# Block order, LayerNorm statistics and early GLU weights in an attention and GLU kernel on one NeuronCore

## The chip, the cores and the metric

The kernel runs on one core of a Trainium2 chip. Five engines work in parallel, each on its own list of instructions in order: TensorE (PE), VectorE (DVE), ScalarE (ACT), GpSimd (POOL) and SyncE (SP), which here only starts DMA transfers. They wait for one another through semaphores. The metric is the device time of one execution in microseconds (us).

## The reference

The input is one sequence of S = 2048 tokens with D = 576 channels, float32. First comes an attention layer, then a gated MLP, each behind a LayerNorm without scale or shift and each added to its input:

```
h  = x + softmax(q k^T * 18**-0.5 over the keys s, s-2, .. s-14) v @ wo    q, k, v = layernorm(x) @ wqkv, 32 heads of 18
h2 = h + (sigmoid(n @ w_gate) * (n @ w_up)) @ w_down                       n = layernorm(h), F = 4608
```

## The kernel before, in words

**Blocks.** A key lies an even number of tokens back, so even and odd tokens never meet. Each half of them is cut in two, which gives four blocks of 512 tokens (0 and 1 even, 2 and 3 odd). A block is held as four token tiles of 128 (the loops over j). The 32 heads are four groups g of 8 (144 channels).

**Precision.** Each product is built of fp32r matmuls: an operand is split into a high part (a copy on ACT, L104) and a low part (the rest, a subtraction on DVE, L105), and three products are summed. L108 and L109 do the same for the last 64 channels. A split is thus always an ACT instruction and a DVE instruction that waits for it.

**The front half** (up to some 223 us). For a block, SP loads x (`load_x`); `ln1` normalizes each token tile with `ln_j`, transposes it on PE (`tr_main`, `tr_rest`) and splits it into the operands th and tl. `ln_j` takes mean and variance with bn_stats and bn_aggr on DVE (L123, L124), the power -1/2 on POOL (L126), and applies them on DVE (L134, L135) or, for blocks 2 and 3, on ACT (L130 to L132). `qkv(b, g)` is four passes (one for each j) of 14 matmuls of 432 columns; the results are evicted by ACT (L384, to ev) and stored to DRAM from ACT's DMA queue (L388, L390).

**Attention** is a generator (`att_all`) that VectorE works off piece by piece while PE runs the passes: for each (block, group) in the order (0,0), (0,1), (1,0), (0,2), (0,3), (1,1), (1,2), (1,3) it loads q, kw and vw (L169 to L171, SP), then does two products pr (L182) and their sums lg (L186), mx, sub, Exp on ACT (L194 to L196), and the weighted sum of v (L208 to L219). `step(ag, n)` lets it advance n pieces for each qkv pass. Blocks 2 and 3 have their attention later, under the GLU. For block 0 the result is a tile of tokens; for the others it is stored by POOL (L221) and loaded again (oj, L570).

**The order of qkv passes** is written out by hand: `norm_under(b, xb, call, n)` interleaves the norm of block b with the passes of `call`, and `heads` lists the passes that follow. `raw_w` and `qkv_w` load and split the weights of a group.

**`front`** then projects block 0 by wo, adds x, normalizes and builds the GLU operands of block 0. It runs between the last qkv passes, (2,3) and (3,3). Its last act is a store of the transposed block (`x<-tok`, ACT queue, L505).

**The GLU** runs over 108 items (a weight chunk for one block or for a pair of blocks; the first 14 are chunks for block 0 alone). An item of the first kind is two products b of 14 matmuls, a sigmoid on ACT (L653), a product on DVE (L629) and a split into h0h and h0l, then the down projection dp (L723). Its weights come as one row of 928 KB (wg), which `weights` splits into w1, w4, w2 and the down part d one item ahead, and `load_gu` loads two items ahead. Chunk 0 is an exception: it is loaded into a tile of the front half (wg0) and `first_split` splits it there to wf, since the pools of the GLU (gw, gd and others) take over memory of the front half (tok, x, weights) and must wait until it is free. A tile in reused memory waits for the last reader of what lay there.

**Background.** While items run, attention (1,2) and (1,3), and after that the projection of block 1 (transposes of oj, L139), go on in their gaps.

**What sets the order within an engine.** A scheduler places instructions by their order in the code and by `tc.high_priority`: a higher number lifts the instructions in it over others that could go at that point.

Of the kernel before, what the change touches and what calls it, by code (L numbers as in the profile page):

```python
# [15 lines left out]
F32 = mybir.dt.float32  # L16
# [5 lines left out]
P = 128  # L22
# [38 lines left out]
def kernel(ctx, tc, x, wqkv, wo, wmlp, out):  # L61
# [53 lines left out]
                sp.dma_start(bass.AP(tensor=a.tensor, offset=a.offset,  # L115
                                     ap=[[LP * CG // 16, 16], [1, LP * CG // 16]]), zero)

    def ln_j(xj, xn, on_act):
        bs = sm.tile([P, 2, 6], F32, bufs=4, name="bs")
        mv = sm.tile([P, 2], F32, bufs=4, name="mv")  # L120
        rstd = sm.tile([P, 1], F32, bufs=4, name="rstd")
        for k in range(2):
            dve.bn_stats(bs[:, k], xj[:, k * DH2:(k + 1) * DH2])  # L123
        dve.bn_aggr(mv, bs)  # L124
        dve.tensor_scalar(rstd, mv[:, 1:2], EPS, None, ALU.add)
        pool.tensor_tensor(rstd, rstd, mhalf, ALU.pow)  # L126
        if on_act:
            nm = sm.tile([P, 1], F32, bufs=4, name="nm")
            dve.tensor_scalar(nm, mv[:, 0:1], -1.0, None, ALU.mult)
            act.activation(xn[:, :D], xj, AF.Identity, bias=nm)  # L130
            act.activation(xn[:, :D], xn[:, :D], AF.Copy, scale=rstd)
            act.activation(xn[:, D:DX], xn[:, DM:D], AF.Copy)  # L132
        else:
            dve.tensor_scalar(xn[:, :D], xj, mv[:, 0:1], rstd, ALU.subtract, ALU.mult)  # L134
            dve.tensor_copy(xn[:, D:DX], xn[:, DM:D])  # L135

    def tr_main(ps, xn):
        for c in range(4):
# [101 lines left out]
    def proj_j(bank, t, wos, th, tl, xn_tile, put, order=(0, 1)):  # L240
        oj = t[0]
        pv = tr_main(bank(), oj)
        with tc.high_priority(HI):
            split(th[:, 0:4], tl, pv)
        yield
        pv = tr_rest(bank(), oj)
        with tc.high_priority(HI):
            split_rest(th[:, 4], pv)
        yield
        for i in order:  # L250
            ps = bank()
            tok_major(ps, DH2, th, tl, slice(0, P), *wos[i])
            hs = t[1][:, i * DH2:(i + 1) * DH2]
            with tc.high_priority(HI):
                dve.tensor_tensor(hs, hs, ps[:, :DH2], ALU.add)
            yield
        xn = xn_tile()
        with tc.high_priority(HI):
            ln_j(t[1], xn, False)
# [62 lines left out]
    def tok_tile(shape=(P, NS, DX)):  # L322
        return stk.tile(list(shape), F32, tag="tok", bufs=2, name="tok")
# [7 lines left out]
    def load_x(b):  # L331
        e, hf = BLOCKS[b]
        t = sah.tile([P, NS, D], F32, bufs=2, name="h")
        for j in range(NS):
            sp.dma_start(t[:, j], xv[e, hf][:, j])
        return t

    def ln1(b, xb):
        th = th3_tile(F32R) if b == 3 else th_tile()
        tl = tl_tile()  # L340
        yield th, tl
        xn = tok_tile()
        for j in range(NS):
            js = slice(j * P, (j + 1) * P)
            pri = 2 * HI if b == 0 else HI if b > 1 else 0
            with tc.high_priority(pri):
                ln_j(xb[:, j], xn[:, j], b > 1)
# [76 lines left out]
    def norm_under(b, xb, call, n):  # L424
        gl = ln1(b, xb)
        T.append(next(gl))
        for _ in call:
            step(ag, n)
            next(gl, END)
            step(ag, n)  # L430
        drain(gl)

    def heads(order, ws, n):
        for b, g in order:
            for _ in qkv(b, g, T[b], ws[g]):
                step(ag, n)
# [11 lines left out]
    xb = load_x(2)  # L448
    norm_under(2, xb, qkv(1, 0, T[1], w[0]), 1)
    xb = load_x(3)  # L450
    wr = raw_w(2)
    norm_under(3, xb, qkv(2, 0, T[2], w[0]), 1)
    heads(((3, 0),), w, 2)
    w.append(qkv_w(2, wr))
    wr = raw_w(3)
    pads(2)
    heads(((1, 1), (0, 2), (2, 1), (3, 1)), w, 2)
    w.append(qkv_w(3, wr))
    pads(3)
    h = load_x(0)  # L460
# [58 lines left out]
    fr = front()  # L519
    for _ in qkv(1, 3, T[1], w[3]):  # L520
        step(ag, 1 if ready else 4)
    while not ready:
        step(ag, 1)
    more = qkv(2, 3, T[2], w[3])
# [15 lines left out]
                ww = first_split(wg)  # L540
    with tc.high_priority(HI):
        drain(fr)
    ps_stk.close()
    sa_stk.close()

# [429 lines left out]
    items = ([("std", 0, f) for f in range(NSTD)] + [("pair", 0, f) for f in range(NSTD, NF)]  # L975
             + [("std", 1, f) for f in range(NSTD)] + [("pair", 1, f) for f in range(NF)])
    bg = under_first()
    with tc.high_priority(2 * HI):
        wg2 = load_gu(1, pool)
        d = d_tile()  # L980
        split(d[:, 0], d[:, 1], wg[:, GU:WC])
        wc = ww, d
    wg = wg2
    seg = []

    def last_pair(i):
# [123 lines left out]
    for c, (kind, p, f) in enumerate(items):  # L1110
# [11 lines left out]
        if c == NF + NSTD:  # L1122
# [4 lines left out]
            X = Xn  # L1127
            pp_stk.close()
            dw = ctx.enter_context(sb_pool("dw", "right"))
        if c + 1 < len(items):  # L1130
            wc = weights(items[c + 1][0], wg, c + 1 < NF + NSTD)
        if c + 2 < len(items):
            wg = load_gu(items[c + 2][2], n=WC if c + 2 < NF + NSTD else GU)
# [94 lines left out]
```

## Time and profile before

| | us |
|---|---|
| three timed runs | 1587.89, 1590.72, 1589.88 (median 1589.88) |
| profiled execution, from its first to its last instruction | 1589.2 |
| TensorE busy in it | 1553.3 |
| VectorE busy | 1268.1 |
| ScalarE busy | 869.2 |

The profile is one execution of its own, and the trace gives its span as its time. A row of the timeline has a start, a length, the engine, the line of the kernel, the operation, the tile written <- the tiles read, their shapes, and how many instructions of the same kind follow each other; in brackets stands the idle time of the engine just before and what ended it. PEld are weight loads, which run beside PE's matmuls; SPq, ACTq and POOLq are DMA issues on these engines' queues. PEclk is the granted clock of TensorE as a share of the full one.

### The profile page before, as it was taken

How to read it: one execution, taken by the hardware profiler on the slowest of the kernel's cores; microseconds unless marked ns; L12 is line 12 of the kernel's file. 1: busy time of each engine (PE TensorE's matmuls, PEld its weight loads, DVE VectorE, ACT ScalarE, POOL GpSimd, SP SyncE). 2: the span in 40 equal slices, each digit the busy share in tenths (PEclk: the TensorE clock that was granted, in tenths of full speed). 3: DMA queues.
4: the chain of work that ended last, by engine and by line, in shares of the span. 5: the costliest groups of instructions: out<-in, count | busy, mean ns of one | idle time of the engine just before them, and what ended most of it. 6: DMA issues, size and time to landing. Idle time of an engine off the chain costs nothing.

```text
span 1589.2 us, 22383 instructions
## 1 busy us (share of the span) xinstructions
PE 1553.3 (98%) x8532; PEld 1381.6 (87%) x8532; DVE 1268.1 (80%) x1931; ACT 869.2 (55%) x1546; POOL 184.2 (12%) x230
## 2 busy tenths in 40 slices
PE   7999979999999999999989999999999999999998
PEld 6999968888888888888879988888888888888887
DVE  7999988959999999999546687876677776677755
ACT  4432234425555666656443255776677776677761
POOL 1000000011010001000101100122112112212210
PEclk9999999999999999999999999999999999999999
DMA  7664544346367565665764234899989999989983
GB/s 267 208 206 163 193 184 165 133 177 246 104 164 205 157 170 139 166 191 149 210 203 143 100 110 110 182 186 181 176 169 183 184 173 180 177 170 182 184 170 124
DMA packets 76892, 273.50 MB, mean 172 GB/s; under 512 B 8336, under 2 KB 14224, under 8 KB 75888
## 3 DMA queue, kind: packets, MB, share of 16 engines
q0 software_dynamic: 27792, 105.89, 36.3%
q1 hardware_dynamic: 41360, 146.06, 27.4%
q10 hardware_dynamic: 7632, 20.12, 3.3%
q8 instruction: 67, 1.10, 0.3%
q14 instruction: 41, 0.34, 0.1%
HBM read 145.88 MB, written 128.52 MB: 173 GB/s over the span
## 4 chain that ended last, share of the span: by engine, by line
PE 55%; issue 27%; POOL 7%; DVE 6%; DMA 4%; ACT 1%; SPq 0%; POOLq 0%; ACTq 0%; DVEq 0%
PE b L609 23%; PE dp L723 15%; POOL h L794 7%; PE acc L150 6%; PE b L616 4%; PE b L150 1%; PE bgp L150 1%; DMA wg<-in_wmlp_dram 1%; DVE pr L182 1%; DMA x<-tok 1%; DVE pr L208 1%; DVE lg L186 1%; PE acc L152 1%; DMA tail<-h 1%; PE acc L153 1%
## 5 line engine op out<-in xcount | busy, mean ns | idle before, releaser
L609 PE MATMUL b<-tl,w 128*128 128x512 f32 x1716 | 438.1, 395 | 9.1 <-ACT w L104 6.5
L609 PEld LDWEIGHTS b<-tl,w 128*128 128x128 f32 x1716 | 311.7, 189 | 66.5 <-ACT w L104 7.7
L609 PE MATMUL b<-th,w 128*128 128x512 f32 x1368 | 352.8, 393 | 0.4 <-DVE s L698 0.3
L609 PEld LDWEIGHTS b<-th,w 128*128 128x128 f32 x1368 | 249.8, 188 | 46.7 <-DVE s L698 0.7
L104 ACT ACTIVATE w<-wg 128x640 fp32r<-128x640 f32 (+2 forms) x197 | 117.0, 598 | 125.2 <-PE b L616 59.8
L791 ACT ACTIVATE ev<-dp 128x576 f32<-128x576 f32 x224 | 145.0, 647 | 61.8 <-PE dp L785 58.2
L616 PE MATMUL b<-th,w 128*128 128x512 f32 x572 | 177.0, 391 | 0.0
L794 POOL DMA_DIRECT2D h<-ev x128 | 110.2, 862 | 456.8 <-ACT ev L791 440.5
L105 DVE TENSOR_TENSOR w<-wg,w 128x640 fp32r<-128x640 f32 (+2 forms) x197 | 126.8, 649 | 38.7 <-ACT w L104 38.3
L150 PE MATMUL acc<-qw,th 128*128 128x432 f32 x512 | 155.7, 365 | 1.2 <-DVE th L109 0.9
L105 DVE TENSOR_TENSOR w<-tw,w 128x512 fp32r<-128x512 f32 x116 | 79.6, 687 | 81.1 <-ACT w L104 80.2
L616 PEld LDWEIGHTS b<-th,w 128*128 128x128 f32 x572 | 107.7, 188 | 23.1
L723 PE MATMUL dp<-d,h0h 128*128 128x288 f32 x640 | 119.0, 296 | 1.7 <-DVE tail L733 1.7
L723 PE MATMUL dp<-d,h1h 128*128 128x288 f32 x640 | 120.0, 297 | 0.0
L723 PEld LDWEIGHTS dp<-d,h0h 128*128 128x128 f32 x640 | 99.4, 189 | 5.5 <-DVE tail L733 2.0
L150 PEld LDWEIGHTS acc<-qw,th 128*128 128x128 f32 x512 | 97.2, 190 | 6.5 <-DVE th L109 1.1
L723 PEld LDWEIGHTS dp<-d,h1h 128*128 128x128 f32 x640 | 99.5, 190 | 2.9
L731 ACT ACTIVATE stage<-dp 128x576 f32<-128x576 f32 x96 | 61.7, 646 | 62.4 <-PE dp L723 62.3
L104 ACT ACTIVATE w<-tw 128x512 fp32r<-128x512 f32 x116 | 72.8, 628 | 41.3 <-PE b L609 40.9
L150 PE MATMUL acc<-qw,tl 128*128 128x432 f32 x256 | 92.8, 362 | 0.0
L384 ACT ACTIVATE ev<-acc 128x432 f32<-128x432 f32 x64 | 33.9, 531 | 104.4 <-PE acc L153 97.7
L182 DVE TENSOR_TENSOR pr<-kw,q 128x2304 f32<-128x2304 f32 x32 | 81.7, 2552 | 2.8 <-DMA kw<-k 2.6
(278 smaller groups left out, 2899.8 us busy)
## 6 DMA issues: line engine op xcount, KB each, us to landing
h<-ev POOLq DMA_DIRECT2D x96, 576.0 KB, 7.2
wg<-in_wmlp_dram SPq DMA_DIRECT2D x49, 928.0 KB, 5.2
h<-stage POOLq DMA_DIRECT2D x24, 1152.0 KB, 10.6
wg<-in_wmlp_dram SPq DMA_DIRECT2D x36, 640.0 KB, 4.1
kw<-k SPq DMA_DIRECT2D x16, 792.0 KB, 4.4
vw<-v SPq DMA_DIRECT2D x16, 792.0 KB, 5.5
wd<-in_wmlp_dram SPq DMA_DIRECT2D x18, 576.0 KB, 7.2
h<-ev POOLq DMA_DIRECT2D x32, 288.0 KB, 6.8
```

The lines of the kernel that those rows point to most:

```text
L104: act.activation(hi, src, AF.Copy)
L105: splits.append(dve.tensor_tensor(lo, src, f32(hi), ALU.subtract))
L150: pe.matmul(ps[:, :n], a[:, c, js], m[:, c], start=k == 0, stop=False)
L152: pe.matmul(ps[:, :n], th[:, 4, js], wh[:, 4], start=False, stop=False)
L182: dve.tensor_tensor(pr, both(kw, u), q[:, us].unsqueeze(2).broadcast_to([P, 2, W, CG]), ALU.mult)
L384: act.activation(ev[:, :, j], ps[:, :NQ].rearrange("p (t c) -> p t c", t=3), AF.Copy)
L609: pe.matmul(ps, wt[:, a, k0 + c], xx[:, m + c], start=first and k == 0, stop=k == 5, skip_group_check=True)
L616: pe.matmul(ps, wt[:, a, k0], xx[:, 4], start=False, stop=a == 1, skip_group_check=True)
L723: pe.matmul(ps[:, i, :DH2], a[:, js], d[:, m, i * DH2:(i + 1) * DH2], start=k == 0, stop=k == n)
L731: act.activation(hv, ps, AF.Copy)
L791: act.activation(hs[:, k % 2], ps[:, :, :DH2], AF.Copy)
L794: pool.dma_start(hsev[:, u, k0:k + 1], hs[:, :k + 1 - k0], accum_op=ALU.add, max_dma_last_dim=8 * D)
```

## The change

It has three parts.

1. **Norm statistics of blocks 2 and 3 go to ScalarE.** The new `ln_stats` takes the negative mean (a Copy with accum_out) and the sum of squared deviations (a Square with accum_out) on ACT, then three small operations on POOL. `ln_scale` applies them in one ACT instruction (Identity with bias and scale) and copies the last 64 channels. Statistics are issued one token tile ahead; the priority of this work falls from HI to 0. bn_stats, bn_aggr and two small DVE operations per token tile go.
2. **qkv(1,1) runs under the norm of block 3** instead of qkv(2,0), and qkv(2,0) follows it; the raw weights of group 2 are loaded after that norm's loads in the code.
3. **Chunk 1 of the GLU is handled like chunk 0.** Its row is loaded on SP into a tile "h" of the front half, after the passes of (1,3) are emitted, and split (`first_split`) before the front's stacks close. The down parts of chunks 0 and 1 are split there too, into tiles df. The POOL-queue load of chunk 1 and the split of chunk 0's d in gd go; the loop takes the ready weights for chunk 1.

```diff
+    def ln_stats(xj, junk):
+        mv = sm.tile([P, 2], F32, bufs=4, name="mv")
+        rstd = sm.tile([P, 1], F32, bufs=4, name="rstd")
+        act.activation(junk[:, :D], xj, AF.Copy, scale=-1.0 / D, accum_out=mv[:, 0:1])
+        act.activation(junk[:, :D], xj, AF.Square, bias=mv[:, 0:1], accum_out=mv[:, 1:2])
+        pool.tensor_scalar(rstd, mv[:, 1:2], 1.0 / D, EPS, ALU.mult, ALU.add)
+        pool.tensor_tensor(rstd, rstd, mhalf, ALU.pow)
+        pool.tensor_tensor(mv[:, 0:1], mv[:, 0:1], rstd, ALU.mult)
+        return mv[:, 0:1], rstd
+
+    def ln_scale(xj, nr, xn):
+        act.activation(xn[:, :D], xj, AF.Identity, bias=nr[0], scale=nr[1])
+        act.activation(xn[:, D:DX], xn[:, DM:D], AF.Copy)
...
     xb = load_x(3)
+    norm_under(3, xb, qkv(1, 1, T[1], w[1]), 1)
     wr = raw_w(2)
-    norm_under(3, xb, qkv(2, 0, T[2], w[0]), 1)
-    heads(((3, 0),), w, 2)
+    heads(((2, 0), (3, 0)), w, 2)
     w.append(qkv_w(2, wr))
     wr = raw_w(3)
     pads(2)
-    heads(((1, 1), (0, 2), (2, 1), (3, 1)), w, 2)
+    heads(((2, 1), (0, 2), (3, 1)), w, 2)
...
     for _ in qkv(1, 3, T[1], w[3]):
         step(ag, 1 if ready else 4)
+    with tc.high_priority(HI):
+        wg1 = sah.tile([P, NS, D], F32, bufs=2, name="h").rearrange("p j d -> p (j d)")[:, :WC]
+        sp.dma_start(wg1, wmlp[1])
...
+    def first_down(ws):
+        d = xt.tile([P, 2, D], F32R, tag="tl", bufs=4, name="df")
+        split(d[:, 0], d[:, 1], ws[:, GU:WC])
+        return d
+
+    with tc.high_priority(HI):
+        wc = ww, first_down(wg)
+        wc_next = first_split(wg1), first_down(wg1)
     ps_stk.close()
     sa_stk.close()
...
-    with tc.high_priority(2 * HI):
-        wg2 = load_gu(1, pool)
-        d = d_tile()
-        split(d[:, 0], d[:, 1], wg[:, GU:WC])
-        wc = ww, d
-    wg = wg2
...
-        if c + 1 < len(items):
+        if c == 0:
+            wc = wc_next
+        elif c + 1 < len(items):
             wc = weights(items[c + 1][0], wg, c + 1 < NF + NSTD)
```

How this moves instructions shows best at three places. The rows name the line, the operation and tile<-tiles; lines of the new kernel differ from the old, so L182 of before is L189 now, L186 is L193, L653 is L678.

On SP, where the front half issues the loads of blocks 2 and 3 (h<-in_x_dram) and of the first attention (q, kw, vw), before:

```order
14 L335 DMA h<-in_x_dram 128x576 x4
15 L362 DMA wr<-in_wqkv_dram 128x432 x5
16 L115 DMA k_2_77<-zero 16x63
17 L115 DMA v_2_85<-zero 16x63
18 L115 DMA k_2_81<-zero 16x63
19 L115 DMA v_2_89<-zero 16x63
20 L115 DMA k_3_78<-zero 16x63
21 L169 DMA q<-q_0_91 128x576
22 L170 DMA kw<-k_0_75 128x1584
23 L171 DMA vw<-v_0_83 128x1584
24 L335 DMA h<-in_x_dram 128x576 x4
```

and now:

```order
14 L342 DMA h<-in_x_dram 128x576 x4
15 L375 DMA wr<-in_wqkv_dram 128x432 x5
16 L342 DMA h<-in_x_dram 128x576 x4
17 L176 DMA q<-q_0_91 128x576
18 L177 DMA kw<-k_0_75 128x1584
19 L178 DMA vw<-v_0_83 128x1584
```

The loads of block 3 stood behind those of the first attention and now stand ahead of them.

On VectorE, at the start of `front`, where tl is the first low part of the transposed attention result, before:

```order
196 L219 TENSOR_TENSOR tok<-kw 128x4x144
197 L182 TENSOR_TENSOR pr<-kw,q 128x2304
198 L409 COPY tok<-tok 128x64 x4
199 L186 TENSOR_REDUCE lg<-pr 128x128
200 L105 TENSOR_TENSOR tl<-mm,th 128x4x128
```

and now:

```order
173 L226 TENSOR_TENSOR tok<-kw 128x4x144
174 L189 TENSOR_TENSOR pr<-kw,q 128x2304
175 L105 TENSOR_TENSOR wow<-ws,wow 128x288 x2
176 L422 COPY tok<-tok 128x64 x4
177 L193 TENSOR_REDUCE lg<-pr 128x128
178 L189 TENSOR_TENSOR pr<-kw,q 128x2304
179 L193 TENSOR_REDUCE lg<-pr 128x128
180 L201 TENSOR_REDUCE mx<-lg 128x32
181 L202 TENSOR_TENSOR lg<-lg,mx 128x256
182 L105 TENSOR_TENSOR tl<-mm,th 128x4x128
```

Between the tile of tokens and tl stood one lg of attention (1,1); now lg, pr, lg, mx and sub stand there.

On ScalarE, from the store of x to the weights of the item after next, before (d is chunk 0's down part, w_2276 to w_2280 are chunk 1's weights, s is the sigmoid of chunk 0):

```order
180 L505 DMA x_113<-tok 128x2560
181 L384 ACTIVATE ev<-acc 128x3x144
182 L388 DMA q_3_106<-ev 128x576
183 L390 DMA k_3_82<-ev 128x576
184 L104 ACTIVATE d<-wg_2056 128x576
185 L390 DMA v_3_90<-ev 128x576
186 L653 ACT_TABLE_LOAD
187 L653 ACTIVATE s<-b_2291 128x512
188 L104 ACTIVATE w_2276<-wg 128x640
189 L104 ACTIVATE w_2279<-wg 128x384
190 L104 ACTIVATE w_2280<-wg 128x256
```

and now (wf and df<-h are chunk 1's, w_2316 is chunk 2's):

```order
197 L518 DMA x_113<-tok 128x2560
198 L397 ACTIVATE ev<-acc 128x3x144
199 L104 ACTIVATE wf<-h 128x256
200 L401 DMA q_3_106<-ev 128x576
201 L403 DMA k_3_82<-ev 128x576
202 L403 DMA v_3_90<-ev 128x576
203 L104 ACTIVATE wf<-h 128x384
204 L104 ACTIVATE df<-h 128x576
205 L203 ACTIVATE lg<-lg 128x256
206 L678 ACT_TABLE_LOAD
207 L678 ACTIVATE s<-b_2256 128x512
```

Chunk 1's weights stood behind the sigmoid of chunk 0 and now stand ahead of it, and so does an Exp of attention (lg), which stood behind them. On PE, the transposes of oj (L139 before, L146 now) stood at the 1553rd matmul and stand at the 1485th.

More of the change, by code (lines that the diff above doesn't have):

```diff
@@ L116, in pads, with ln_j @@
                                      ap=[[LP * CG // 16, 16], [1, LP * CG // 16]]), zero)
-    def ln_j(xj, xn, on_act):
+    def ln_j(xj, xn):
         bs = sm.tile([P, 2, 6], F32, bufs=4, name="bs")
@@ L126, in ln_j @@
         pool.tensor_tensor(rstd, rstd, mhalf, ALU.pow)
[L127 to L135, printed above, removed]
+        dve.tensor_scalar(xn[:, :D], xj, mv[:, 0:1], rstd, ALU.subtract, ALU.mult)
+        dve.tensor_copy(xn[:, D:DX], xn[:, DM:D])
+    def ln_stats(xj, junk):
[10 more added lines that the diff above has]
+        act.activation(xn[:, D:DX], xn[:, DM:D], AF.Copy)
     def tr_main(ps, xn):
@@ L258, in proj_j @@
         with tc.high_priority(HI):
-            ln_j(t[1], xn, False)
+            ln_j(t[1], xn)
         yield
@@ L342, in ln1 @@
         xn = tok_tile()
+        pri = 2 * HI if b == 0 else 0
+        nr = []
         for j in range(NS):
             js = slice(j * P, (j + 1) * P)
-            pri = 2 * HI if b == 0 else HI if b > 1 else 0
+            while b > 1 and len(nr) < min(j + 2, NS):
+                nr.append(ln_stats(xb[:, len(nr)], xn[:, len(nr)]))
             with tc.high_priority(pri):
-                ln_j(xb[:, j], xn[:, j], b > 1)
+                if b > 1:
+                    ln_scale(xb[:, j], nr[j], xn[:, j])
+                else:
+                    ln_j(xb[:, j], xn[:, j])
             pv = tr_main(mm_tile(), xn[:, j])
```

## The prediction

> **What bounds the kernel now.** I read the page first, then the split of the span into windows, then the list of waits, and last the timeline at the places the list names.
>
> ```profile
> span 1589.2 us, 22383 instructions
> PE 1553.3 (98%) x8532; PEld 1381.6 (87%) x8532; DVE 1268.1 (80%) x1931; ACT 869.2 (55%) x1546; POOL 184.2 (12%) x230
> ```
>
> TensorE is busy for 1553.3 of 1589.2 us, and the diff leaves its matmuls alone. So the change can only move the 35.9 us in which PE stands still, and the stretches in which it runs at a lower granted clock. The list of waits over the whole span says who causes the first (the columns are the total, the count and the longest):
>
> ```profile
> PE b L609 <- ACT w L104: 6.5, 1, 6.5
> PE b L609 <- DVE s L629: 2.5, 1, 2.5
> PE b L139 <- DMA oj<-o: 2.4, 1, 2.4
> ```
>
> The windows of 5 us show the second (PE busy, PEld, DVE, ACT, POOL, then PEclk, DMA share, GB/s):
>
> ```profile
> 235.00:240.00 5.00, 1.46 (x3) 0.78 (x4) 4.93 (x4) 3.59 (x7) 0.00 (x0) 0.50 0.11 41
> 240.00:245.00 5.00, 5.00 (x13) 3.98 (x14) 4.73 (x9) 0.27 (x1) 0.00 (x0) 0.50 0.16 30
> 245.00:250.00 5.00, 5.00 (x22) 4.07 (x21) 1.42 (x3) 3.35 (x6) 0.00 (x0) 0.91 0.42 160
> 250.00:255.00 5.00, 5.00 (x28) 4.39 (x27) 4.97 (x7) 4.09 (x6) 0.00 (x0) 1.00 0.63 215
> 320.00:325.00 5.00, 5.00 (x26) 4.54 (x25) 2.07 (x4) 1.79 (x3) 0.00 (x0) 0.66 1.02 402
> ```
>
> At 250 us PE does 28 matmuls in 5 us; at 240 us, just as busy, it does 13, because the clock was granted at 0.50. The rows of the timeline tell what happened (start, length, and in brackets the idle time before and who ended it):
>
> ```profile
> 222.95 1.56 PE L609 MATMUL b<-tl,wf 128*128 128x512 f32 x6
> ...
> 228.89 0.61 PE L616 MATMUL b<-th,wf 128*128 128x512 f32 x2
> 232.36 0.68 ACT L104 ACTIVATE d<-wg 128x576 fp32r<-128x576 f32 x1 [8.68 <-DMA x<-tok]
> ...
> 233.06 1.28 ACT L653 ACT_TABLE_LOAD   x1
> ...
> 233.75 2.55 DVE L182 TENSOR_TENSOR pr<-kw,q 128x2304 f32<-128x2304 f32 x1
> 234.36 0.60 ACT L653 ACTIVATE s<-b 128x512 f32<-128x512 f32 x1
> ...
> 236.03 1.22 PE L609 MATMUL b<-tl,w 128*128 128x512 f32 x2 [6.52 <-ACT w L104]
> 236.34 2.55 DVE L186 TENSOR_REDUCE lg<-pr 128x128 f32<-128x2304 f32 x1
> ...
> 239.76 1.19 PE L609 MATMUL b<-tl,w 128*128 128x512 f32 x2 [2.50 <-DVE s L629]
> ...
> 242.69 2.77 PE L609 MATMUL b<-th,w 128*128 128x512 f32 x6
> ```
>
> GLU chunk 0 ends at 229.5. Chunk 1 needs weight halves that ScalarE makes, and ScalarE stands before d of chunk 0 for 8.68 us, until the store of x has landed and freed the memory in which d lies. Then PE waits 6.52 us, later 2.50 us more, and six matmuls take 2.77 us instead of 1.56. From 240 to 250 it does 35 matmuls where 56 fit at the rate of 250 to 255: 3.8 us, of which I put 0.7 down to the shorter mix of work. **The hand-over from chunk 0 to chunk 1 costs 6.5 + 2.5 + 3.1 = 12.1 us.** It is a third of PE's standstill, and the change is aimed at the front half of the program, where it lies.
>
> **The change, part by part.** The sum is made against the profiled execution (1589.2 us; the median of the three runs is 1589.88, 0.7 above).
>
> *Hand-over.* In the new order, chunk 1's halves wf and both df stand in tiles of xt, before the stacks close. None waits for the store of x; the first that does is d of chunk 2, on ScalarE, with a whole chunk in hand. So 6.5 goes. What is late next is VectorE: between the front's last tiles and the sigmoid's product stand five halves and four pieces of attention (1,2). The pieces: pr 2.55 and lg 2.55 from the rows above, mx and sub from these:
>
> ```profile
> 243.12 0.61 DVE L194 TENSOR_REDUCE mx<-lg 128x32 f32<-128x256 f32 x1
> ...
> 244.32 0.41 DVE L195 TENSOR_TENSOR lg<-lg,mx 128x256 f32<-128x256 f32 x1
> ```
>
> That is 6.1 us. The halves, taken like the row of d (0.7 each), are 3.5. Together 9.6, against 6.5 us that PE spends in chunk 0: PE lacks about 3 us. ScalarE has on its queue, ahead of chunk 0's sigmoid, the Exp that waits for sub, then the table load of 1.28 us and the sigmoid's 0.60. I take a stall of 2.6 us; the ends are 0 (all of it under chunk 0) and 5.0 (Exp, load and sigmoid in a row behind sub). For the clock I take 1.2: 320 to 325 shows 26 matmuls at 0.66 after a wait of 2.4, and its neighbour at 1.00 does 28 to 31. The ends are 0 and 3.1. Left: 3.8 of 12.1, so **−8.3** (−12.1 to −4.0).
>
> The Trainium skill ("TensorE: Matmul & The Clock Gate", Part 1) says that the clock halves after an idle window of about 3.4 us. By that page a stall of 2.6 would cost no clock, and the sum would be 1.2 lower. The 0.66 after 2.4 us of idle disagrees. The skill's "ScalarE: Activation LUTs" (What ACT_TABLE_LOAD costs) adds a drain of 1.38 us to each load; by it the stall would grow to some 4 us. Here the sigmoid at 234.36 follows a load that ends at 234.34, so the trace has none.
>
> *Front.* Here the moved attention costs. The rows of before at the projection's start:
>
> ```profile
> 35.95 2.56 DVE L182 TENSOR_TENSOR pr<-kw,q 128x2304 f32<-128x2304 f32 x1 [2.58 <-DMA kw<-k]
> ...
> 184.41 2.54 DVE L186 TENSOR_REDUCE lg<-pr 128x128 f32<-128x2304 f32 x1
> ...
> 186.98 0.69 DVE L105 TENSOR_TENSOR tl<-mm,th 128x512 fp32r<-128x512 f32 x1
> ...
> 187.73 0.40 PE L150 MATMUL mm<-wo,th 128*128 128x288 f32 x1 [1.33 <-DVE tl L105]
> ```
>
> VectorE makes tl behind one lg; in the new order behind lg, pr, lg, mx and sub, 6.1 us more, plus two halves of wo (0.4 each, an estimate from mx and sub, rows of like size): +6.9. Against that, work that stood between its first pr and this place is gone:
>
> ```profile
> 40.24 0.82 DVE L123 BATCH_NORM_STATS2 bs<-h 128x6 f32<-128x288 f32 x2
> ...
> 42.14 0.14 DVE L125 TENSOR_SCALAR rstd<-mv 128x1 f32<-128x1 f32 x1
> ```
>
> Block 3's statistics are 8 of 0.41 and 12 of about 0.14, less a few hundredths of overlap each, 4.6 us. Two tl and two th (0.69 and some 0.3) come ahead of the first pr, 2.0, and two halves of wo go behind, 0.8: −7.4. The first pr itself starts later, since on SP q, kw and vw of attention (0,0) now stand behind the four loads of block 3:
>
> ```profile
> 31.19 0.34 SPq L170 DMA_DIRECT2D kw<-k  x1
> ...
> 33.11 2.33 SPq L335 DMA_DIRECT2D h<-in_x_dram  x4
> ```
>
> The kw issue came 1.9 us before these and would come after their 2.33 us; block 1's norm, which frees the loads' memory, ends about 1.3 earlier without the statistics between. I take pr at 38.9, +3.0 (0 to +5). So tl comes 6.9 − 7.4 + 3.0 = 2.5 us later. The transposes of the new h stand 8 matmuls nearer to what they wait for; before, PE waits there 0.45 and 0.28:
>
> ```profile
> 210.79 0.66 PE L139 MATMUL mm<-ident,tok 128*128 128x128 f32 x4 [0.45 <-DVE tok L134]
> ...
> 220.11 0.46 PE L150 MATMUL acc<-qw,th 128*128 128x432 f32 x1 [0.28 <-ACT ev L384]
> ```
>
> I add 0.5 (0 to 1.5, with 8 matmuls of 0.18). **+3.0** (−0.5 to +6).
>
> *Norms of blocks 2 and 3.* Per token tile VectorE loses about 1.1 us. ScalarE goes from two passes of 576 and a short copy to three and a copy, POOL from one instruction to three:
>
> ```profile
> 30.78 1.44 ACT L130 ACTIVATE tok<-h,nm 128x576 f32<-128x576 f32 x2
> ```
> ```profile
> 31.91 2.62 POOL L126 TENSOR_TENSOR rstd<-rstd,mhalf 128x1 f32<-128x1 f32 x5 [2.16 <-DVE rstd L125]
> ```
> ```profile
> 20.00:40.00 20.00, 20.00 (x111) 18.95 (x110) 15.51 (x52) 11.46 (x27) 4.27 (x8) 1.00 0.87 303
> 40.00:60.00 20.00, 18.88 (x109) 17.42 (x108) 19.44 (x40) 13.77 (x32) 2.20 (x4) 1.00 0.75 253
> ```
>
> ScalarE gains 8 × 0.72 = 5.8 us and is busy for 25.2 of these 40, so its work fits; PE's matmuls cover it. If that cover fails, each tile shows its chain: Square, three POOL operations of 0.55, Identity. The trace has no accumulating ACTIVATE and no other POOL arithmetic of this size; pow is the nearest row, and the ends are 0 and 1.1 us per tile. I expect 0.8 us of waiting, and it is swallowed: PE waits for tl at the front in any case, at a time that VectorE sets. **0** (−1 to +9).
>
> *Chunk 2's down projection* waits for a half that is now behind a pr of 2.55: **+0.7** (0 to 2.5).
>
> *Where attention (1,3) ends.* The rows of before:
>
> ```profile
> 233.08 0.76 DVE L105 TENSOR_TENSOR d<-wg,d 128x576 fp32r<-128x576 f32 x1 [4.34 <-ACT d L104]
> ...
> 310.18 0.75 DVE L219 TENSOR_TENSOR kw<-kw 128x576 f32<-128x576 f32 x1
> ...
> 311.86 0.82 POOL L223 DMA_DIRECT2D o<-kw  x1
> ...
> 319.78 0.66 PE L139 MATMUL b<-ident,oj 128*128 128x128 f32 x4 [2.40 <-DMA oj<-o]
> ```
>
> From the end of attention to its transposes lie 8.8 us of store and load. In the new order these transposes stand 68 matmuls earlier on PE, 12 us at 28 per 5 us, and PE comes 4.6 us sooner: 16.6. VectorE has fewer pieces of the GLU ahead of its last one (in the order, one pr and lg, mx, sub, eight halves and five sums less), about 15 us by the lengths above, and loses the wait for d in this row; less 2.5 at the front: 16.8. The two cancel, and the stall of 2.4 with its slow clock stays: **0** (−4 without it, +4.5 if VectorE gains less).
>
> *Sum:* −8.3 + 3.0 + 0 + 0.7 + 0 = −4.6 us, or 1584.6 for the span and 1585.3 for the median. I round to **1585.5**.
>
> **Rivals.**
> 1. *All of the hand-over is won.* For it: five of nine pieces ahead of the sigmoid have time under the last passes of block 3, and the first pr might not move. Against: 9.6 us of VectorE's work stand against 6.5 of PE's. Then −12.1 + 0 + 0.7, or 1578.5.
> 2. *The change does not do what it says:* the hand-over's wait is replaced, not removed. Exp waits for sub, the table load stands behind it, and the stall is 5.0 with 2.5 of slow clock (−4.6), while the front's +3.0, 0.7 and 0.4 at (1,3) remain: −0.5, about 1589.
> 3. *Slower: the statistics' chain on ScalarE and POOL comes onto PE's path* in blocks 2 and 3. Its queue holds evictions and Exp between the links, and PE waits for tok as it did here for th. At the two added POOL operations, 8 × 1.1 = 8.8 us, the sum is +4.2 and the time 1594. It decides from 4.6 + 3.2 = 7.8 us on, about 1 us per tile. Against: stats are issued one tile ahead, and ScalarE is idle a third of that time.
>
> **How the numbers follow.** Forecast 0.43, first rival 0.22, second 0.16, third 0.19. A measurement of this kernel can tell about 0.2%, 3.2 us, from no change. Forecast and first rival are faster than that (0.65), the second is the same (0.16), the third slower (0.19). The range leaves out half of the first rival and half of the third: 1577 to 1594. The forecast's own range is 1582 to 1587.
>
> **What would show it.** Right: no wait of ScalarE for the store of x ahead of chunk 1, PE idle under 4 us at the hand-over, PEclk near 1.00 by 245 us; PE waiting 3 to 4 us for tl at the front instead of 1.33; the first pr near 39 us; still a wait for oj near 303. Wrong: waits of PE for tok or th between 40 and 70 us that add up to more than 3 us; an Exp and a table load that end later than 236; a front that starts at 187.7 as before; no wait for oj, or one over 5 us.

## The result and the profile after

| | before | after |
|---|---|---|
| median of 12 runs each, same chip | 1589.45 us | 1589.26 us |
| lowest and highest | 1586.87, 1593.26 | 1586.48, 1593.5 |
| profiled span | 1589.2 us | 1588.0 us |

The ratio is 0.9998, with a 95% interval of 0.999 to 1.0005: **no change**. The forecast of 1585.5 was not met; the time lies inside the range.

The page of the kernel after, its span and the busy times:

```profile
span 1588.0 us, 22369 instructions
PE 1553.6 (98%) x8532; PEld 1381.1 (87%) x8532; DVE 1262.2 (79%) x1891; ACT 872.7 (55%) x1568; POOL 193.7 (12%) x245
```

TensorE's work is the same; POOL gained 15 instructions and 9.5 us. The list of PE's waits in the kernel after (total, count, longest):

```profile
PE mm L146 <- ACT tok L141: 2.6, 1, 2.6
PE mm L157 <- DVE tl L105: 1.8, 1, 1.8
PE acc L150 <- ACT tok L142: 1.8, 2, 1.0
PE dp L748 <- DVE h0l L105: 1.6, 1, 1.6
...
PE b L634 <- ACT s L678: 1.5, 1, 1.5
PE acc L157 <- DVE qw L105: 1.2, 1, 1.2
```

The two waits of the hand-over, 6.5 and 2.5, are gone, and so is the wait for oj. What is on top now are six shorter rows, two of them for ScalarE in the norms (tok at L141 and L142 is what `ln_scale` writes). The timeline of the kernel after at the hand-over:

```profile
231.58 1.55 PE L634 MATMUL b<-tl,wf 128*128 128x512 f32 x6
...
237.19 0.42 ACT L203 ACTIVATE lg<-lg 128x256 f32<-128x256 f32 x1 [0.88 <-DVE lg L202]
...
237.63 1.28 ACT L678 ACT_TABLE_LOAD   x1
...
238.93 0.60 ACT L678 ACTIVATE s<-b 128x512 f32<-128x512 f32 x1
...
239.58 1.65 PE L634 MATMUL b<-tl,wf 128*128 128x512 f32 x6 [1.46 <-ACT s L678]
```

Exp waits for sub, then come the table load and the sigmoid, as predicted, and PE stands 1.46 us. But chunk 0 starts at 231.58 and not at 222.95. The windows of 40 to 80 us say where PE fell behind (PE busy and its matmuls, PEld, DVE, ACT, POOL, then PEclk), of before:

```profile
40.00:80.00 40.00, 38.88 (x218) 36.48 (x217) 38.79 (x61) 19.70 (x46) 2.20 (x4) 1.00 0.60 208
```

and of after:

```profile
40.00:80.00 40.00, 35.66 (x191) 33.03 (x191) 38.85 (x40) 24.12 (x62) 11.29 (x18) 0.96 0.59 203
```

In the same 40 us PE does 27 matmuls fewer. At 40/218 = 0.183 us each that is an estimated 5.0 us. And POOL, whose 18 instructions are a few tenths of a microsecond each when alone, is busy for 11.29 us. The timeline of the kernel after at its longest wait for tok:

```profile
64.28 2.56 DVE L215 TENSOR_TENSOR pr<-vw,lg 128x2304 f32<-128x2304 f32 x1
...
64.78 2.10 POOL L135 TENSOR_SCALAR rstd<-mv 128x1 f32<-128x1 f32 x1 [1.53 <-ACT tok L134]
...
66.97 0.55 POOL L136 TENSOR_TENSOR rstd<-rstd,mhalf 128x1 f32<-128x1 f32 x1
67.60 0.19 POOL L137 TENSOR_TENSOR mv<-mv,rstd 128x1 f32<-128x1 f32 x1
67.82 0.87 ACT L141 ACTIVATE tok<-h,mv,rstd 128x576 f32<-128x576 f32 x1 [2.37 <-POOL mv L137]
68.74 1.12 PE L146 MATMUL mm<-ident,tok 128*128 128x128 f32 x4 [2.58 <-ACT tok L141]
```

Read it from the bottom: PE waits for tok, ScalarE for mv, mv stands behind rstd on POOL, and rstd, one number for each of 128 partitions, takes 2.10 us. It ends at 66.88, just after VectorE's product pr, which ends at 66.84. The same line takes 0.19 us when no such product runs. From this came the theory to test.

The ledger of the two profiled spans, in us (after less before):

| stretch | how read | difference |
|---|---|---|
| start to the wo product (187.73, now 194.51) | 27 matmuls 5.0, wait for qw 1.2, wait for tl 1.77 − 1.33 | +6.8 |
| wo product to chunk 0 (35.2, now 37.1) | starts of the rows | +1.9 |
| chunk 0's start to the end of chunk 1's second product (26.0, now 14.9) | starts and ends of the rows | −11.1 |
| behind it | rest of the span's −1.2 | +1.3 |

The first row counts what PE lost; the wo product itself waits for VectorE, and the step-by-step account below comes back to that. So the gain at the hand-over was there, larger than forecast, and was paid back, for the most part before it.

### The profile page after: what moved, and what is told of

It is laid out like the page before. It is cut to its first block, busy times and chain, and to the rows that moved or that the text cites. A ratio compares the mean times of both kernels' runs of the same rounds, so it can differ in the third digit from the quotient of the medians.

```text
span 1588.0 us, 22369 instructions
## 1 busy us (share of the span) xinstructions
PE 1553.6 (98%) x8532; PEld 1381.1 (87%) x8532; DVE 1262.2 (79%) x1891; ACT 872.7 (55%) x1568; POOL 193.7 (12%) x245
## 4 chain that ended last, share of the span: by engine, by line
PE 86%; DVE 8%; DMA 3%; ACT 1%; issue 1%; POOL 1%; SPq 0%; ACTq 0%; DVEq 0%; POOLq 0%
PE b L634 41%; PE dp L748 14%; PE dp L810 11%; PE b L641 8%; PE acc L157 7%; PE b L157 1%; PE bgp L157 1%; DMA wg<-in_wmlp_dram 1%; DVE lg L193 1%; DVE pr L215 1%; DVE w L105 1%; PE acc L160 1%; PE acc L159 1%; DVE tl L105 1%; DVE pr L189 1%
## 5 line engine op out<-in xcount | busy, mean ns | idle before, releaser
L634 PE MATMUL b<-tl,w 128*128 128x512 f32 x1704 | 432.4, 393 | 0.0
L634 PEld LDWEIGHTS b<-th,w 128*128 128x128 f32 x1356 | 247.0, 188 | 46.7 <-DVE s L723 1.3
L104 ACT ACTIVATE w<-wg 128x384 fp32r<-128x384 f32 (+2 forms) x194 | 115.7, 598 | 119.8 <-PE b L641 59.4
L105 DVE TENSOR_TENSOR w<-wg,w 128x384 fp32r<-128x384 f32 (+2 forms) x194 | 125.2, 650 | 38.1 <-ACT w L104 38.0
L641 PEld LDWEIGHTS b<-th,w 128*128 128x128 f32 x568 | 106.7, 188 | 23.4
L748 PE MATMUL dp<-d,h0h 128*128 128x288 f32 x608 | 112.5, 295 | 0.8 <-DVE tail L758 0.8
L748 PEld LDWEIGHTS dp<-d,h0h 128*128 128x128 f32 x608 | 93.6, 189 | 3.9 <-DVE tail L758 1.0
L189 DVE TENSOR_TENSOR pr<-kw,q 128x2304 f32<-128x2304 f32 x32 | 81.7, 2552 | 3.2 <-DMA kw<-k 3.0
```

The lines of the kernel that those rows point to most:

```text
L104: act.activation(hi, src, AF.Copy)
L105: splits.append(dve.tensor_tensor(lo, src, f32(hi), ALU.subtract))
L189: dve.tensor_tensor(pr, both(kw, u), q[:, us].unsqueeze(2).broadcast_to([P, 2, W, CG]), ALU.mult)
L634: pe.matmul(ps, wt[:, a, k0 + c], xx[:, m + c], start=first and k == 0, stop=k == 5, skip_group_check=True)
L641: pe.matmul(ps, wt[:, a, k0], xx[:, 4], start=False, stop=a == 1, skip_group_check=True)
L748: pe.matmul(ps[:, i, :DH2], a[:, js], d[:, m, i * DH2:(i + 1) * DH2], start=k == 0, stop=k == n)
```

## The experiments

The theory: part 1 costs PE about 5 to 9 us, because its chain passes POOL beside VectorE's products; parts 2 and 3 are worth what they seem. The rivals: the loss comes from the order (part 2); part 3 gains little by itself; or what PE waits for is ScalarE's list, on which the norms stand in line with other work. All results in one table. "Chunk 0" is the start of its first matmul; "hand-over" is from there to the end of chunk 1's second product, both in the profiled execution.

| parts of the change | ratio to before (95%) | chunk 0 | hand-over |
|---|---|---|---|
| none (before) | 1 | 222.95 | 26.0 |
| 1 | 1.0006 (0.9997 to 1.0014) | 228.37 | 20.1 |
| 2 | 1.0005 (0.9996 to 1.0014) | 223.28 | 26.6 |
| 3 | 0.9953 (0.9942 to 0.9965) | 222.76 | 19.6 |
| 2, 3 | 0.9948 (0.9936 to 0.9959) | 222.55 | 19.2 |
| 1, 3 | 0.9992 (0.9984 to 1.0001) | 227.92 | 18.6 |
| 1, 2 | 1.0027 (1.0016 to 1.0037) | 230.80 | 20.9 |
| 1, 2, 3 (after) | 0.9998 (0.999 to 1.0005) | 231.58 | 14.9 |
| 1, 2, 3, statistics two tiles ahead | 0.9986 (0.9977 to 0.9995) | 229.51 | 14.9 |
| 2, 3, one product held | 0.9915 (0.9901 to 0.9928) | 221.76 | 12.9 |
| 3, one product held | 0.9903 (0.9886 to 0.9921) | 223.01 | 12.9 |
| 1, 2, 3, one product held | 0.9973 (0.9961 to 0.9985) | 233.58 | 13.3 |

**Part 1 alone.** Of the kernel after, the order of the passes and the early weights are undone:

```diff
-    norm_under(3, xb, qkv(1, 1, T[1], w[1]), 1)
     wr = raw_w(2)
-    heads(((2, 0), (3, 0)), w, 2)
+    norm_under(3, xb, qkv(2, 0, T[2], w[0]), 1)
+    heads(((3, 0),), w, 2)
...
-        wc = ww, first_down(wg)
-        wc_next = first_split(wg1), first_down(wg1)
```

> Part 1 alone (statistics of blocks 2 and 3 on ScalarE and POOL), order and weights as before. Theory A, the chain of statistics is what delays the front half: PE waits for normalized tok tiles between 45 and 75 us, 3 us or more in all with a low clock behind the longest, chunk 0 starts 4 to 7 us later than 222.95, the hand-over still costs 12, and the kernel is 4 to 7 us slower (about 1595). Theory B, the new order of passes and loads is what delays it: no such waits over 1 us, chunk 0 starts within 1.5 us of 222.95, time within 1.5 us of before.

The window of 40 to 80 us, with part 1 alone, shows the whole loss of the kernel after:

```profile
40.00:80.00 40.00, 36.25 (x191) 33.30 (x190) 38.86 (x40) 23.10 (x59) 7.39 (x16) 0.96 0.62 201
```

191 matmuls again, and chunk 0 starts 5.4 us late. PE waits for tok here too, 2.04 and 1.49 us, and only the shorter wait has a held POOL operation ahead of it (1.28 us at L135). The longer one is for the copy of the last 64 channels (L142). It stands on ScalarE behind an Exp, which had waited 2.98 us for VectorE, three issues of stores and evictions. So not all of the loss is POOL's: part of it comes from ScalarE's list, where an instruction that waits holds up all behind it. The timeline of this kernel:

```profile
54.95 0.42 ACT L203 ACTIVATE lg<-lg 128x256 f32<-128x256 f32 x1 [2.98 <-DVE lg L202]
...
58.57 0.26 ACT L142 ACTIVATE tok<-tok 128x64 f32<-128x64 f32 x1
...
58.89 0.33 PE L150 MATMUL acc<-ident,tok 128*128 128x128 f32 x1 [2.04 <-ACT tok L142]
```

Yet the time is that of before, not the 4 to 7 us more that were expected: the hand-over gives the 5.4 us back (20.1 for 26.0). PE comes later to the wait for w and waits 4.99 for 6.52, and the second wait, 2.5, is gone. PE's row there, with part 1 alone:

```profile
239.91 3.17 PE L622 MATMUL b<-tl,w 128*128 128x512 f32 x6 [4.99 <-ACT w L104]
```

**Part 2 alone.** `ln_j` with on_act and the old weights, but the new order:

```diff
     xb = load_x(3)
+    norm_under(3, xb, qkv(1, 1, T[1], w[1]), 1)
     wr = raw_w(2)
-    norm_under(3, xb, qkv(2, 0, T[2], w[0]), 1)
-    heads(((3, 0),), w, 2)
+    heads(((2, 0), (3, 0)), w, 2)
```

> Part 2 alone ((1,1) under block 3's norm, first attention's loads behind block 3's), norms and weights as before. Theory A: chunk 0 starts 0 to 3 us later than 222.95 and the time is 0 to 3 us above before. Theory B: chunk 0 starts 5 us or more later, and the time is 4 to 7 us above before.

The window of 40 to 80 us with part 2 alone:

```profile
40.00:80.00 40.00, 38.82 (x216) 36.11 (x215) 38.77 (x62) 19.66 (x46) 2.19 (x4) 1.00 0.61 207
```

216 matmuls and chunk 0 0.3 us late: the order by itself does nothing. What the prediction put into the front comes with part 1. The first pr starts at 37.05 here, and at 38.93 with part 1 alone: with part 1 the loads of block 3 stand ahead of those of the first attention on SP, with the old order of passes too. They are issued once block 1's norm has read its last tile of h: at 28.81 after 28.79 with part 1 alone, at 33.11 after 33.08 before. The five pieces of VectorE ahead of tl, too, stand there in every kernel with part 1, alone or not, and in none without it. Beside part 1, though, the order is not free: parts 1 and 2 together take 1.0027, with chunk 0 2.4 us later than with part 1 alone; tl is 1.7 us later (192.97 for 191.27).

**Part 3 alone, and parts 2 and 3.**

```diff
+    with tc.high_priority(HI):
+        wc = ww, first_down(wg)
+        wc_next = first_split(wg1), first_down(wg1)
     ps_stk.close()
```

> Part 3 alone (chunk 1's weights and both down parts split before the stacks close), norms and order as before. Both theories: PE's wait of 6.5 us for ScalarE's w is gone and the hand-over from chunk 0 to the end of chunk 1 takes 13 to 17 us instead of 26, of which a wait behind an attention product may give 2 to 3 back; chunk 0 starts within 1 us of 222.95. Time 6 to 10 us below before, about 1581. If it is no faster, the gain at the hand-over is taken back later whatever the front does, by the wait for attention (1,3) or by VectorE.

> Parts 2 and 3 without part 1: the changed kernel with the old norms of blocks 2 and 3. Theory A: chunk 0 starts at 223 to 226 and the time is 4 to 9 us below both before and the changed kernel, about 1582. Theory B: chunk 0 starts at 228 or later, time as before.

Early weights alone take 7.5 us off the time (0.0047 of 1590), within the expected 6 to 10, though the hand-over takes 19.6 us where 13 to 17 were expected. Both kernels have their last stall at one place; the timeline with part 3 alone:

```profile
233.54 2.54 DVE L186 TENSOR_REDUCE lg<-pr 128x128 f32<-128x2304 f32 x1
...
236.11 0.69 DVE L641 TENSOR_TENSOR s<-s,b 128x512 f32<-128x512 f32 x1
...
236.85 2.93 PE L621 MATMUL b<-tl,wf 128*128 128x512 f32 x6 [4.38 <-DVE s L641]
```

The sigmoid had ended at 228.48; its product s on VectorE stands behind what is left of one lg, then wf, pr, df and the next lg, 7.6 us in all, and PE waits 4.38 us and then runs slower (six matmuls in 2.93 for 1.52). This is the new wait in place of the old one.

**Parts 1 and 3; parts 1 and 2.** They complete the square; the edits are those above.

> Parts 1 and 3 without part 2. If the norms' delay and the weights' gain simply add, the time is that of the weights alone plus the 1 us of the norms alone, about 1585. Theory A (late front: chunk 0 starts near 228, and what the norms lost at the front is no longer given back at the hand-over, since no wait is left there to hide it): about 1587 to 1589, as the changed kernel. The rival says that only the order together with the norms does harm: then 1584 to 1585.

> Parts 1 and 2 without part 3. If the hand-over of before hides a late front (its length falls from 26 to 20 when chunk 0 starts 5.4 us later, as with part 1 alone), chunk 0 starts at 228 to 231, the hand-over takes 18 to 21 and the time is 0 to 3 us above before. If nothing hides it, the time is 6 to 9 us above before.

Parts 1 and 3 take as long as the kernel after, so the harm needs no order. Parts 1 and 2 have the chunk 0 and the hand-over that were expected, but lie 4 us above before where 0 to 3 were. What part 1 costs, by differences of the ratios: on before 0.0006, on part 2 0.0022, on part 3 0.0039, on parts 2 and 3 0.0050. That is 1.0, 3.5, 6.2 and 8.0 us (of 1590), each to some 2 us by the intervals. Where the hand-over waits for the store of x the cost mostly disappears in that wait; where the weights are early it is paid.

**Statistics two tiles ahead.** If the chain is too long, starting it earlier should help:

```diff
-            while b > 1 and len(nr) < min(j + 2, NS):
+            while b > 1 and len(nr) < min(j + 3, NS):
```

> The changed kernel with statistics issued two token tiles ahead instead of one. If the length of the chain (Square, three POOL operations, Identity) is what PE waits for, the waits for tok between 45 and 75 us fall from 4.3 to under 2 us and the time by 2 to 5. If the number of instructions on ScalarE's queue is what it waits for, the same work stands on the queue earlier, the waits stay at 3 to 6 us and the time stays or grows.

It takes some 2 us off (0.9986), which the intervals hardly tell from nothing, and not what the chain costs. The timeline of this kernel:

```profile
55.41 0.42 ACT L203 ACTIVATE lg<-lg 128x256 f32<-128x256 f32 x1 [2.90 <-DVE lg L202]
...
59.72 0.86 ACT L141 ACTIVATE tok<-h,mv,rstd 128x576 f32<-128x576 f32 x1
...
60.64 0.86 PE L146 MATMUL mm<-ident,tok 128*128 128x128 f32 x4 [3.79 <-ACT tok L141]
...
63.14 0.54 POOL L135 TENSOR_SCALAR rstd<-mv 128x1 f32<-128x1 f32 x1 [0.58 <-ACT tok L134]
63.66 2.56 DVE L215 TENSOR_TENSOR pr<-vw,lg 128x2304 f32<-128x2304 f32 x1
63.76 2.87 POOL L136 TENSOR_TENSOR rstd<-rstd,mhalf 128x1 f32<-128x1 f32 x1
```

Now the power at L136 falls beside a product and takes 2.87 for its usual 0.55 us. It ends 0.41 after the product. But PE does not wait for it. PE waits once, 3.79 us up to 60.64, for another tile, whose last POOL operation had ended by 53.69. Its Identity (59.72) stands on ScalarE behind an Exp that waited 2.90 us for VectorE, evictions, and statistics of the tiles that follow. So the waits stay between 3 and 6 us, as the second reading had it for ScalarE's list, and PE does 192 matmuls between 40 and 80 us where the kernel after does 191, though no held POOL operation makes it wait.

**No attention beside the norms.** Nothing is left out; the first attention starts only when the last tl of block 3 is made. A copy of one element into q, which the load of q overwrites, makes it wait:

```diff
+        if (b, g) == (0, 0):
+            dve.tensor_copy(q[:, 0, 0:1], f32(T[3][1][:, 0, TB - 1:TB]))
...
-    norm_under(2, xb, qkv(1, 0, T[1], w[0]), 1)
+    norm_under(2, xb, qkv(1, 0, T[1], w[0]), 0)
...
-    norm_under(3, xb, qkv(1, 1, T[1], w[1]), 1)
+    norm_under(3, xb, qkv(1, 1, T[1], w[1]), 0)
```

> The changed kernel with the first attention held back until block 3's last low part is made, so that no product pr runs on VectorE beside the norms. Theory A1, a POOL operation beside pr cannot end before pr does: all eight POOL operations of L135 take 0.2 us (three took 1.76 to 2.45 in the changed kernel), and PE waits for tok under 1.5 us in all between 45 and 75 us. Rival A2, ScalarE's queue is too full: the waits for tok stay at 3 us or more. The end comes 10 us or more later in both, since VectorE starts its attention some 30 us later.

The group of L135 in this kernel, and then its window of 40 to 80 us:

```profile
L135 POOL TENSOR_SCALAR rstd<-mv x8: 183/190/192, 28.3 to 60.5; 128x1 f32<-128x1 f32 x8
```

```profile
40.00:80.00 40.00, 39.50 (x219) 37.23 (x218) 16.42 (x22) 23.77 (x60) 4.64 (x15) 1.00 0.48 165
```

All eight take 183 to 192 ns (in the kernel after the longest took 2446), PE does 219 matmuls and waits once for tok, 0.49 us. ScalarE does as much as in the kernel after, 23.77 for 24.12 us. So the statistics on ScalarE cost PE nothing there by themselves; they cost it while VectorE works at attention. The time of this kernel (1602.51 in one run) says nothing of that, since VectorE starts late and PE waits 15.59 us for it at 201 us. The edit takes away more than the hold on POOL: the pieces ahead of tl on VectorE, and the Exp on ScalarE that other waits for tok stood behind. So it does not tell these causes apart; the next run looks at the hold alone.

**The hold by itself.** Before, with 241 small POOL instructions that nobody reads, from attention (1,0) on:

```diff
+        if (b, g) == (1, 0):
+            pool.tensor_scalar(probe, q[:, 0, 0:1], 1.0 / D, EPS, ALU.mult, ALU.add)
+            for _ in range(240):
+                pool.tensor_scalar(probe, probe, 1.0 / D, EPS, ALU.mult, ALU.add)
```

> The kernel before with 241 POOL operations of 128x1 in a row, from attention (1,0) on; they add nothing to the outputs. Theory A1: one lasts 0.2 us beside VectorE's reductions lg (one operand from memory) and until the end of the product beside pr (two operands), up to 2.5 us; so about one operation ends per pr. Rival: their lengths do not follow what VectorE runs.

Two windows of this kernel, POOL alone (busy, count), beside the sum lg and beside the product pr<-vw,lg:

```profile
87.70:89.60 1.90, 1.32 (x8) 1.00 0.02 4
94.60:97.00 2.40, 2.32 (x2) 1.00 1.01 347
```

Eight of these instructions fit into 1.9 us beside lg; in 2.4 us beside pr there are two, one of which fills the window. Counted over all 241 by what VectorE did when each began:

| VectorE meanwhile | count | POOL instruction |
|---|---|---|
| nothing | 142 | 0.19 us |
| sums over one tile (lg) | 45 | 0.19 us, one 1.23 |
| pr<-vw,lg | 6 | 2.39 to 2.51 us |
| pr<-kw,q | 4 | 2.37 to 2.39 us |
| pr<-pr, added halves | 6 | 1.19 to 1.31 us |
| kw<-pr | 6 | 0.59 to 0.71 us |

The other 32 began beside shorter instructions; 16 of them beside two SBUF operands, and these were held too. An instruction that begins beside a VectorE instruction with two operands in SBUF ends 0.04 to 0.05 us after it, whatever is left of it. Two that began up to 0.1 us ahead of such an instruction took 1.23 and 0.92 us. VectorE loses nothing: its products take 2.55 to 2.57 us here and 2.55 to 2.56 before. In the kernel after, POOL instructions beside tl<-mm,th, which has one operand in PSUM, are not held so (0.55 us at 41.60, 0.19 at 49.05). The Trainium skill ("GPSIMD Engine Reference", 1. Specifications) says that GpSimd shares its SBUF interfaces with VectorE and contends with instructions that have two SBUF inputs; these rows agree. The hold is one of the two things that the prediction's working on the norms left out. (The run's time, 1630.17, is that of 241 instructions on a queue that also stores attention, and bears on nothing.)

**One product held.** If VectorE's order is the last stall at the hand-over, the second pr of attention (1,2) has to stand behind the product of chunk 0's sigmoid. With parts 2 and 3:

```diff
+                if (b, g, u) == (1, 2, 1):
+                    while not gate:
+                        yield
+                    pin.enter_context(tc.issue_after(getattr(gate[0], "ins", gate[0])))
                 pr = at.tile([P, 2, W, CG], F32, name="pr")
...
-        dve.tensor_tensor(sg, sg, ps, ALU.mult)
+        gate.append(dve.tensor_tensor(sg, sg, ps, ALU.mult))
```

> Parts 2 and 3 (as in the run without part 1), and the second product pr of attention (1,2) placed on VectorE behind the gated product s of chunk 0. If the order on VectorE is what is left of the hand-over (PE waited 4.06 us for s, which stood behind pr, a half and lg, then ran six matmuls in 2.85 us), that wait falls under 1.5 us, the hand-over from 19.2 to 14 to 15, and the time by 3 to 5 more, to about 0.992 of before. Rival: the pieces only move, the wait returns at chunk 1's product or at the down projection, and the time stays within 1.5 us of the run without part 1.

The timeline of this kernel's VectorE:

```profile
230.21 0.69 DVE L647 TENSOR_TENSOR s<-s,b 128x512 f32<-128x512 f32 x1
230.81 2.55 DVE L188 TENSOR_TENSOR pr<-kw,q 128x2304 f32<-128x2304 f32 x1
```

s now comes first, PE waits nowhere in the hand-over, which takes 12.9 us, and PEclk stays at 1.00 from 225 to 250. The ratio is 0.9915. The same with all three parts, and with part 3 alone:

> All three parts of the change, with the second product of attention (1,2) held behind chunk 0's sigmoid product as in the run before. Theory: the statistics' chain delays TensorE by 5 to 9 us before chunk 0, and nothing behind it gives that back once the hand-over no longer waits. Then chunk 0 starts near 231.5, the hand-over takes about 13 us, the 4th group ends near 244.5, and the ratio is 0.995 to 0.998. Rival: the delay stands against waits that VectorE's pieces cause later in any case; then the 4th group ends at 235 to 238 and the ratio is 0.991 to 0.993, as without part 1.

> Part 3 alone with the same product held. Theory: the order of the passes (part 2) is worth nothing, so the times are those of parts 2 and 3 with the product held: chunk 0 at 222 to 223, hand-over 12.5 to 13.5 us, ratio 0.990 to 0.993. Rival: the order is what lets the product be held without harm, since it puts the passes of (1,1), on which attention (1,1) waits, earlier; then waits for VectorE or for oj come up elsewhere and the ratio is 0.994 or above.

With part 1 the hand-over is just as short (13.3), but chunk 0 comes at 233.58, and the ratio is 0.9973: here part 1 costs 0.0058, 9.2 us, in full. Without the new order (part 3 alone) the ratio is 0.9903, and its page reads:

```profile
span 1573.5 us, 22376 instructions
PE 1546.8 (98%) x8532; PEld 1377.7 (88%) x8532; DVE 1267.7 (81%) x1931; ACT 868.3 (55%) x1546; POOL 183.2 (12%) x229
```

This is the best kernel found, 1575.78 us against 1591.31 of before in the same job: early weights, one product held, and nothing else of the change. Its interval overlaps that of parts 2 and 3 with the product held, so no worth of the order is shown here either.

## Why the prediction was right and wrong, step by step

The time lies inside the range, but the gain of 4.6 us that the sum forecast did not come, and one step failed in its mechanism. That the range holds is in part luck: an error of 2.8 us at the hand-over and a larger one ahead of it have opposite signs.

- **Norms of blocks 2 and 3: 0, "swallowed". This step failed.** PE lost an estimated 5.0 us in the window of 40 to 80. The prediction bounded each added POOL operation by pow, 0.55, but its length depends on what VectorE does beside it, up to 2.45 us in the kernel after; one of 2.10 is behind the longest wait for tok, 2.58. And it took the total of ScalarE's idle time for cover, but the norms stand in one list with Exp and evictions; the other two waits, 0.75 and 1.01, are for a copy that stands behind an eviction and splits. The quoted row of pow, 2.62 us for five, showed no hold because none of the five ran beside such a product. The cover at the front failed in part as well. PE does wait for tl there, at a time that VectorE sets, but VectorE had itself been held up by the late PE. The timeline of the kernel after:

```profile
84.36 0.42 DVE L202 TENSOR_TENSOR lg<-lg,mx 128x256 f32<-128x256 f32 x1
...
87.68 0.53 ACT L397 ACTIVATE ev<-acc 128x432 f32<-128x432 f32 x1 [2.22 <-PE acc L160]
...
88.11 0.41 ACT L203 ACTIVATE lg<-lg 128x256 f32<-128x256 f32 x1
...
88.55 0.66 DVE L205 TENSOR_REDUCE rs<-lg 128x32 f32<-128x256 f32 x1 [3.76 <-ACT lg L203]
```

  Sub is done at 84.78. The Exp stands behind an eviction, the eviction waits for a pass of PE, and VectorE stands 3.76 us; before, the wait at this place is 0.49. With PE 5.0 us earlier the eviction would have been over before sub (an estimate). tl starts 6.8 us later than before (193.76 for 186.98): 3.0 from the first pr, 0.6 from VectorE's work between the two (145.12 us for 144.55) and 3.2 from its idle time there (9.73 for 6.48), for which the prediction had nothing. By this estimate some 3.2 us of the step that was put at 0 came through at the front, and the rest was swallowed. With part 1 alone it is less: tl is 4.3 later, by 3.0, 0.7 and 0.6. The cost of part 1 as a whole, 6.2 to 9.2 us with early weights, thus holds the front's late first pr as well.
- **The third rival** named this chain, and its picture, evictions and Exp between the links, is in the rows; the waits for tok between 40 and 70 us add up to 0.75 + 1.01 + 2.58 = 4.3, over the 3 named as the sign. Its price, 8.8, came from two more operations at a fixed length, and that is not how the loss arose.
- **Front: +3.0.** The first pr came at 38.91 for 38.9, and VectorE's work up to tl was near (+0.6 for −0.5). But tl came 6.8 us later, not 2.5, by the idle time above, and from the wo product to chunk 0 it was 1.9, not 0.5. PE's wait for tl was 1.77, not 3 to 4, because PE came late itself.
- **Hand-over: −8.3.** Mechanism right, size off: −11.1. The stall was 1.46, not 2.6, and no slow clock followed (−1.2): the window of 240 to 245 has 1.00. Chunk 0 starts 8.6 us later, and sub comes 5.15 us behind that start. With parts 1 and 3, where it comes 7.57 behind, the same row of Exp, table load and sigmoid stalls PE for 3.87, near the working's upper end of 5.0. Without part 1 the stall is 4.1 to 4.4 with a slow clock, but there it is the product s on VectorE that is late, not the Exp and the table load.
- **Chunk 2's down: +0.7, with 2.5 as its end.** It was 3.5, by the mechanism given, a half behind a product. The timeline of the kernel after:

```profile
252.85 0.68 PE L748 MATMUL dp<-df,h0l 128*128 128x288 f32 x2 [1.62 <-DVE h0l L105]
...
253.81 2.33 PE L634 MATMUL b<-tl,w 128*128 128x512 f32 x5
255.94 1.80 PE L634 MATMUL b<-th,w 128*128 128x512 f32 x6
```

  The wait is 1.62; five matmuls in 2.33 for 1.27, six in 1.80 for 1.52, and two pairs of dp in 0.68 for 0.42 add 1.9.
- **Where attention (1,3) ends: 0.** The stall of 2.4 went; waits of 1.07 and 0.46 for th at 320 us replace it. With chunk 2's 3.5 and the +1.3 of the ledger this place gained some 2 us.
- **The sum.** −4.6 became −1.2 by the spans: 2.8 more won at the hand-over and 2.2 where attention (1,3) ends, against 5.6 more lost ahead of chunk 0 (8.6 for 3.0) and 2.8 at chunk 2. The time is that of the second rival, but not by its mechanism: the hand-over was won nearly as the first rival has it, and the late start of chunk 0 paid it back.
- **The clock.** After 2.58 us of idle, PEclk in the kernel after is 0.87 at 65 to 70 us and 0.78 at 70 to 75, and after 1.62 us at 253 it is 0.81 in the window of 250 to 255. The rule of the Trainium skill ("TensorE: Matmul & The Clock Gate", Part 1), a window of about 3.4 us, does not fit these rows. No price for one wait fits either: a wait of 2.94 us at 68.7 was followed by 1.00 with parts 1 and 3, and one of 2.94 at 68.1 by 0.85 with all parts and the held product (both from 70 to 80 us).

**Open.** No run takes away the hold on POOL and leaves all else, so how the loss in the norms splits between the hold, ScalarE's list and the front's order on VectorE is read from single waits, not measured. Part 1 also lowers the priority of the norms from HI to 0, and no run changes that alone; it may be why the copy stands behind evictions, though without attention beside the norms it cost nothing. A form of the statistics without POOL was not tried. With part 1 there, the order adds 2.4 to 3.7 us at chunk 0. At tl it adds 1.7 and 2.5 of that, and why was not settled; the wait for qw, 1.2 us near 136, ends ahead of a wait for tl that PE has in any case.

## What to carry to other kernels

Price a small operation that moves to another engine by what runs beside it in its new place: here one of 0.19 us took up to 2.5 us beside a large product on VectorE, and it stood in a chain that TensorE waited for. Idle time in sum is no cover for an engine that works off a list in order: look for what can wait ahead of the moved work on that list. When a wait is removed, look in the same kernel for delays that it was hiding, and test the parts of a change one by one: here one part gave 7 us and another took them. And when an operand comes early, ask which short operation behind a long one on the next engine is now last; one product moved behind it was worth another 5 to 8 us.

## What the runs showed of the hardware that was not expected

- A POOL instruction on 128x1 elements that begins beside a VectorE instruction with two SBUF operands ends 0.05 us after that one: 0.19 becomes up to 2.51 us. Beside sums over one tile it stays at 0.19 (241 operations in one run).
- Each accumulating ACTIVATE is followed by a read of the accumulator of 0.20 us on ScalarE, 16 in all, which the prediction had not counted; and Identity with bias and scale as operands takes 0.87 where the passes before, with one such operand, took 0.77.
